# Digits laid out tile by tile, low parts of the first weights on VectorE, and a third place for stacked keys and queries

## The chip, the core and the metric

The kernel runs on one core of a Trainium2 chip. The metric is the device time of one execution in microseconds; a kernel's time is the median of its runs. The engines are TensorE (PE in the profile, its weight loads PEld), VectorE (DVE), ScalarE (ACT), GpSimd (POOL) and SyncE (SP), which issues most DMAs.

## What is computed

Three layers follow each other: attention with queries pooled in pairs (4 batches, 8 heads, 1152 positions, head width 64), a mixture of experts that gives each of 2304 tokens one of 8 experts with a capacity of 288 each, and a gated feed-forward layer of width 1536.

```python
q_pool = q.reshape(B, H, S // 2, 2, D).mean(axis=3)
scores = scale * np.matmul(q_pool, k.transpose(0, 1, 3, 2))
attn = softmax(scores)                      # over the keys
x = (attn @ v) as rows of [2304, 512]
flat = (x @ w_gate).flatten()               # 2304 x 8 logits
for idx in np.argsort(-flat):               # best pair first
    tok, e = idx // E, idx % E
    if assigned[tok] >= 0 or counts[e] >= cap: continue
    assigned[tok] = e; counts[e] += 1
out[mask_e] = relu(x[mask_e] @ w1[e]) @ w2[e]     # per expert
y = (silu(out @ w_gate2) * (out @ w_val)) @ w_out
```

## The kernel before

**Attention** is cut into units: one head of one batch with 576 pooled queries in batches 0 to 2, and in the last batch (`b == B - 1`) twice eight half-units, with 320 and then 256 queries (16 in all). For each of nine key tiles `score` (L351, L352) makes two matmuls into a PSUM bank, `expo` (L373) takes the exponential on ScalarE, `value` (L385) multiplies by the values, `add_weights` (L393, L395) adds the weights of three key tiles on GpSimd, and `sum_weights` (L400) sums them on TensorE into the same bank (`pv`, one buffer). `x_copy` (L414) and `den_copy` (L422) empty that bank. Scores are made in split precision: a stacked tile holds the high part of the keys in rows 64 to 127 twice and the low part in rows 0 to 63 (`ks`), and the queries lie likewise in `qs`, with the negative row maxima in its first two rows (`mrows_mm` L328, `mrows_copy` L333). `stack` (L252 to L256) fills such a tile by five DMAs, in the last batch from the scratch tensors `kh_s`, `kl_s` and `q_s` in DRAM. There are two places for stacked tiles; unit `u` uses place `u % 2`.

The order of all this is written out by a planner (`Plan`): each task has an engine, a duration, a due time, tasks that it comes after, buffers that it takes and frees, and a latency until another engine sees it. The planner always takes the task that can start first, the earliest due time among equals, and the engines' queues follow that order. A stack is a task of 2.0 on SP with a latency of 6.0 (`stlat`); it comes after the one before (`last_st`), and after the buffer is free. Scores of a unit come after its stack. VectorE has fillers: `rank_cmp` (L561, L563) compares one tile of 128 tokens with all tokens up to it for one expert, 2.7 planner microseconds for tile 12, and these are added only while tasks of attention are left.

**The tail** does the comparisons that were not placed: `tail_cmp` on VectorE (L993, L960) with 15 to 18 matmuls that count (L999), some by ScalarE. GpSimd prepares constants at the same time (`pool_steps`), among them `colv`, a grid of column numbers [128, 128, 18] with the token tile innermost.

**The routing rounds** (7 of them) find, for each expert, the rank up to which tokens are taken. A round takes each token's best key (`choose`), splits its rank in two digits, writes for each digit a table of thresholds `onehot` [128, digit value, token tile] by `is_ge` (`up_to`, L1163, four operations, two per digit), counts them by 18 matmuls per digit (`count`, L1171) with 8-column weights, and finds the cut (`cut`, L1177, L1179). Each matmul reads the columns `ths[k][:, :, i]`, which lie 18 elements apart. At the end of six rounds, `rows_after` turns a tile of rows and stores it to `x_rows`.

**Behind the rounds** the places of the tokens are split into digits again (`low_digit` L1267, `high_digit` L1273 and L1274) and 18 matmuls per list (`tokens_of`, L1281) give the gather indices `gidx0`, `gidx1` and the scatter indices `sidx`. `warm_up` (L1289) puts matmuls over 512 columns of `colv` between. Then GpSimd gathers the first expert's rows (L1344), TensorE transposes them (L1349), and the expert matmuls start (`hidden` L1418, `project` L1437).

**The expert weights** are loaded in pieces of 128x1024 (`w_load`, L1324) and split by `w_split`: ScalarE makes the high part (L1332), a subtraction the low part (L1334). The first three pieces are split early, right behind the tail, with both subtractions of each on GpSimd; of the later ones VectorE takes the first half and GpSimd the second.

Instructions outside `manual_schedule` are put in order when the program is built, by readiness and program order. `tc.issue_after(ins)` puts what it encloses behind `ins` on the same engine.

## Time and profile before

| what | us |
|---|---|
| median of 3 runs (1415.59 to 1419.45) | 1418.36 |
| the profiled execution | 1414.83 |
| its span, first to last instruction | 1413.0 |
| TensorE busy in the span | 1318.2 (93%) |
| VectorE busy | 938.4 (66%) |
| ScalarE busy | 612.5 (43%) |
| GpSimd busy | 520.8 (37%) |
| last attention batch, 461.0 to 609.3 | 148.3 |
| tail, 609.3 to 657.4 | 48.1 |
| routing rounds, 657.4 to 716.1 | 58.7 |
| digits and first gather, 716.1 to 728.7 | 12.6 |
| both expert layers, 728.7 to 1413.0 | 684.3 |

A row of the trace begins with the start in microseconds from the start of the span and the duration, then the engine, the line of the kernel, the operation, what is written and read, and the shape; in brackets stands the idle time of the engine before it and what ended that. Ends of matmuls are modelled, and spans on GpSimd are rough.

### The profile page before, as it was taken

The page shows a single profiled execution, that of the slowest core. Times are in us where ns is not written, and L with a number is a line of the kernel's source. Part 1 is how long each engine was busy: PE and PEld are TensorE (multiplying, and loading weights), DVE is VectorE, ACT ScalarE, POOL GpSimd, SP SyncE. Part 2 cuts the span into 40 slices and gives each one's busy share as a digit, 9 for nine tenths or more (in the row PEclk, how much of TensorE's full clock was granted, in tenths as well). Part 3 has the DMA queues.
Part 4 walks back from the last instruction along what each step waited for, and adds up shares of the span by engine and source line. Part 5 has one row for each costly group of instructions (what it writes and reads, how often), then busy time and mean ns, then how long its engine had stood idle before and what let it go on. Part 6 is the DMA issues. An engine that isn't in the chain of part 4 may idle for free.

```text
span 1413.0 us, 26870 instructions
## 1 busy us (share of the span) xinstructions
PE 1318.2 (93%) x10236; PEld 1095.4 (78%) x10237; DVE 938.4 (66%) x1960; ACT 612.5 (43%) x1643; POOL 520.8 (37%) x447
## 2 busy tenths in 40 slices
PE   7999999999999988786679999999999999999997
PEld 5565655666655777676569999999999999999997
DVE  5767688878989899979658888866742323232322
ACT  4556555555545555555226555654321212121211
POOL 7655323333324364553037677755610000000000
PEclk9999999999989999888569999999999999999999
DMA  7656566566643786621037767754310101010000
GB/s 223 190 155 185 134 173 188 126 179 180 188 93 88 194 211 160 155 76 46 38 101 244 241 231 244 255 189 129 90 45 1 45 1 45 1 45 0 23 0 23
DMA packets 78352, 174.43 MB, mean 123 GB/s; under 512 B 8448, under 2 KB 38160, under 8 KB 78224
## 3 DMA queue, kind: packets, MB, share of 16 engines
q1 hardware_dynamic: 75248, 163.29, 40.9%
q0 software_dynamic: 2976, 9.44, 1.8%
q8 instruction: 80, 1.31, 0.4%
q14 instruction: 48, 0.39, 0.1%
HBM read 120.86 MB, written 21.31 MB: 101 GB/s over the span
## 4 chain that ended last, share of the span: by engine, by line
PE 54%; DVE 18%; issue 17%; ACT 4%; POOL 2%; DMA 2%; SPq 1%; POOLq 0%; ACTq 0%; DVEq 0%
PE pv L385 8%; PE py L1437 7%; PE ph L1418 7%; PE st L351 6%; DVE cmp L561 6%; PE pm L282 4%; PE pg L1524 4%; PE misc L1524 4%; PE po L1547 4%; PE st L352 3%; PE pv L400 2%; DVE cmp L563 2%; PE pc L1171 2%; DVE cmp L993 1%; DVE mxp L294 1%
## 5 line engine op out<-in xcount | busy, mean ns | idle before, releaser
L294 DVE TENSOR_REDUCE mxp<-pm 128x1 f32<-128x384 f32 x405 | 199.5, 549 | 73.7 <-PE pm L282 70.7
L373 ACT ACTIVATE Lrow<-st 128x288 f32<-128x288 f32 (+2 forms) x432 | 154.3, 411 | 94.3 <-PE st L352 80.3
L351 PE MATMUL st<-qs,ks 128*128 128x288 f32 (+2 forms) x504 | 171.3, 352 | 9.9 <-ACT Lrow L373 7.0
L561 DVE SCALAR_TENSOR_TENSOR cmp<-Lrow,Lt,cmp 128x384 fp8e4<-128x384 f32 (+8 forms) x145 | 153.2, 1077 | 0.0
L352 PE MATMUL st<-qs,ks 128*128 128x288 f32 (+2 forms) x504 | 149.3, 306 | 3.3 <-ACT qs L333 3.2
L1555 POOL DMA_INDIRECT out_dram<-ot,si x18 | 17.4, 968 | 362.5 <-DVE ot L1552 359.9
L393 POOL TENSOR_TENSOR Lrow<-Lrow 128x576 f32<-128x576 f32 (+2 forms) x50 | 70.3, 1405 | 206.1 <-ACT Lrow L373 203.6
L1535 DVE TENSOR_TENSOR sg<-pg,sg 128x384 f32<-128x384 f32 x72 | 40.1, 556 | 159.4 <-ACT sg L1534 159.4
L351 PEld LDWEIGHTS st<-qs,ks 128*128 128x128 f32 x504 | 99.1, 197 | 49.6 <-ACT Lrow L373 23.7
L385 PE MATMUL pv<-Lrow,v 128*64 128x288 f32 (+2 forms) x900 | 124.9, 415 | 3.4 <-ACT den L422 3.2
L1334 POOL TENSOR_TENSOR wl<-wr,wh 128x512 fp32r<-128x512 f32 x67 | 103.5, 1551 | 59.0 <-ACT wh L1332 30.8
L352 PEld LDWEIGHTS st<-qs,ks 128*128 128x128 f32 x504 | 100.3, 199 | 4.8 <-ACT qs L333 4.8
L1534 ACT ACTIVATE sg<-pg 128x384 f32<-128x384 f32 x72 | 35.3, 491 | 155.4 <-PE pg L1524 155.4
L1537 ACT CAST ah<-ac 128x384 fp32r<-128x384 f32 x72 | 36.9, 513 | 149.2 <-DVE ac L1536 149.2
L1524 PE MATMUL pg<-yl,w2h 128*128 128x384 f32 x288 | 96.9, 337 | 0.1
L1524 PE MATMUL pg<-yh,w2h 128*128 128x384 f32 x288 | 97.0, 337 | 0.0
L1524 PE MATMUL pg<-yh,w2l 128*128 128x384 f32 x288 | 96.8, 336 | 0.0
L1524 PE MATMUL misc<-yh,w2h 128*128 128x384 f32 x288 | 96.8, 336 | 0.0
L1524 PE MATMUL misc<-yl,w2h 128*128 128x384 f32 x288 | 96.8, 336 | 0.0
L1524 PE MATMUL misc<-yh,w2l 128*128 128x384 f32 x288 | 96.8, 336 | 0.0
L385 PEld LDWEIGHTS pv<-Lrow,v 128*64 128x64 f32 x900 | 59.2, 140 | 46.7 <-issue 13.6
L1547 PE MATMUL po<-w2l,ah 128*128 128x512 f32 x216 | 85.5, 396 | 0.0
(281 smaller groups left out, 3465.4 us busy)
## 6 DMA issues: line engine op xcount, KB each, us to landing
wr<-in_wm_dram SPq DMA_DIRECT2D x64, 512.0 KB, 3.6
raw<-in_wm_dram SPq DMA_DIRECT2D x36, 512.0 KB, 4.1
ks<-pkh SPq DMA_DIRECT2D x23, 576.0 KB, 5.6
v<-in_v_dram SPq DMA_DIRECT2D x20, 576.0 KB, 6.3
pk<-in_kT_dram SPq DMA_DIRECT2D x16, 576.0 KB, 5.6
pq<-in_qT_dram SPq DMA_DIRECT2D x32, 288.0 KB, 6.4
Lrow<-l_cols SPq DMA_DIRECT2D x18, 512.0 KB, 5.6
ks<-kh_s SPq DMA_DIRECT2D x16, 576.0 KB, 7.3
```

What stands on the lines that cost most here:

```text
L294: nc.vector.tensor_reduce(mx[:, i, j:j + 1], p[:, :w3], axis=AX.X, op=OP.max)
L351: nc.tensor.matmul(p[:, :w], KS[u][:, 1, ks], QS[u][:, 1, cs_], start=True, stop=False)
L352: nc.tensor.matmul(p[:, :w], KS[u][:, 0, ks], QS[u][:, 0, cs_], start=False, stop=True)
L373: nc.scalar.activation(EX[u, gi, kt][:, ti * w:(ti + 1) * w], ST.pop((u, gi, kt, ti))[:, :w], AF.Exp, scale=SCALE)
L385: nc.tensor.matmul(p[64 * k:64 * k + 64, :hn], VT[u][:, kt, o:o + 64], ex[:, k * hn:(k + 1) * hn], start=(kt == 0), stop=(kt == KT - 1), s ...
L393: nc.gpsimd.tensor_add(w[:, :n], a, b)
L561: nc.vector.scalar_tensor_tensor(c[:, sl], Lrow[:, e, sl], Lt[:, i, e:e + 1], c[:, sl], op0=OP.is_ge, op1=OP.add, accum_out=acc, saturate= ...
L1334: eng.tensor_sub(WL[k][:, s], r[:, s], WH[k][:, s].bitcast(F32))
L1418: nc.tensor.matmul(p[:, :CAP], w[:, cs_], x[:, c, :], start=(n == 0), stop=(n == 11))
L1437: nc.tensor.matmul(PY[e][m][:, :CAP], w[:, ms], h, start=(f == 0 and n == 0), stop=(f == FB1 - 1 and n == 2))
L1524: nc.tensor.matmul(p[:, :TG], w[ft][:, cs_], y[g][:, c, :], start=(n == 0), stop=(n == 11))
L1547: nc.tensor.matmul(PO[g][t], a[:, ts], w[ft][:, 1024:], start=(ft == 0 and n == 0), stop=(ft == FB2 - 1 and n == 2))
```

## The change

Attention: the planner gets a third kind of place, `ks3`, for every third unit of the last batch. It is made of the `kh` and `qh` tiles of two slots in which batches 0 to 2 prepared keys and queries; two memsets on GpSimd set its constant rows. Stacks of the last batch no longer come after the stack before.

Routing: `onehot` is [128, token tile, digit value], so the columns that a matmul reads are neighbours, and `colv` is one row of 128 numbers. The source that holds the digits is repeated over the innermost dimension. `warm_up` reads `onehot`.

Weights: the three early splits are made in rounds 1, 3 and 5, their subtractions on VectorE behind the `nbelow` reductions of this round and the one before.

```diff
+    U3 = next(u for u in range(NU) if units[u][0] == B - 1)
+    third = [u >= U3 and (u - U3) % 3 == 1 for u in range(NU)]
+    place = [sum(not x for x in third[:u]) % BUFS["ks"] for u in range(NU)]
+    def KS(u, k):
+        return slots[1 - k]["kh"] if third[u] else ksbuf[place[u]][:, k]
+    def QS(u, k):
+        return slots[1 - k]["qh"] if third[u] else qsbuf[place[u]][:, k]
+    def third_init():
+        nc.gpsimd.memset(KS(U3 + 1, 0)[:64].bitcast(F32), 1.0)
+        nc.gpsimd.memset(QS(U3 + 1, 0)[:64].bitcast(F32), 0.0)
...
-        nc.sync.dma_start(ks[64:], kh[:, None].to_broadcast([64, 2, S]))
+        if third[u]:
+            for k in range(2):
+                nc.sync.dma_start(ks[k][64:], kh)
+        else:
+            nc.sync.dma_start(ksbuf[place[u]].bitcast(F32)[64:], kh[:, None].to_broadcast([64, 2, S]))
...
+        if u == U3 + 1:
+            ks3_init = [add("POOL", 3.0, up - 16, third_init, (), (buf("prep0"), buf("prep1")))]
...
-            kdep = [add("SP", 2.0, up + PRM["k2due"], lambda u=u, t=t: stack(u, t), ready + last_st, (bks,),
+            kdep = [add("SP", 2.0, up + PRM["k2due"], lambda u=u, t=t: stack(u, t), ready + (last_st if u <= U3 else []) + (ks3_init if third[u] else []), (bks,),
...
-    colv = rst.tile([128, 128, NT], I16, name="colv")
+    colv = rst.tile([128, 128], I16, name="colv")
-    onehot = rst.tile([128, 128, NT], BF, name="onehot")
+    onehot = rst.tile([128, NT, 128], BF, name="onehot")
...
-        for k in range(4):
-            nc.gpsimd.iota(colv[:, k * 32:(k + 1) * 32], pattern=[[1, 32], [0, NT]], base=32 * k, channel_multiplier=0)
-            yield
+        nc.gpsimd.iota(colv, pattern=[[1, 128]], base=0, channel_multiplier=0)
+        yield
...
-            nc.vector.tensor_tensor(ths[k][:, :, sl], grid[:, :n, sl],
-                                    digs[k][:, None, sl].to_broadcast([128, n, HT]), op=OP.is_ge)
+            nc.vector.tensor_tensor(ths[k][:, sl], colv[:, None, :n].to_broadcast([128, HT, n]),
+                                    digs[k][:, sl, None].to_broadcast([128, HT, n]), op=OP.is_ge)
...
-            nc.tensor.matmul(p[:E, :n], who[:, i, :], ths[k][:, :, i], start=(i == 0), stop=(k == 0 and i == NT - 1))
+            nc.tensor.matmul(p[:E, :n], who[:, i, :], ths[k][:, i, :], start=(i == 0), stop=(k == 0 and i == NT - 1))
...
-            eng = nc.vector if a == 0 and not early else nc.gpsimd
-            eng.tensor_sub(WL[k][:, s], r[:, s], WH[k][:, s].bitcast(F32))
+            if early:
+                with tc.issue_after(early[a].ins):
+                    nc.vector.tensor_sub(WL[k][:, s], r[:, s], WH[k][:, s].bitcast(F32))
+            else:
+                eng = nc.vector if a == 0 else nc.gpsimd
+                eng.tensor_sub(WL[k][:, s], r[:, s], WH[k][:, s].bitcast(F32))
...
+            ins = nc.vector.tensor_reduce(nbelow, below.rearrange("p i e -> p e i"), axis=AX.X, op=OP.add)
+        told.append(ins)
+        if rnd % 2 and rnd < 2 * WAH:
+            w_split(rnd // 2, told[-2:])
+            w_load(rnd // 2 + LAH - WAH)
...
-            nc.vector.tensor_tensor(ob[:, :, a:b], colv[:, :, a:b], lo[:, None, a:b].to_broadcast([128, 128, b - a]),
-                                    op=OP.is_equal)
+            nc.vector.tensor_tensor(ob[:, a:b], colv[:, None].to_broadcast([128, b - a, 128]),
+                                    lo[:, a:b, None].to_broadcast([128, b - a, 128]), op=OP.is_equal)
...
-            nc.tensor.matmul(p, identb, colv[:, :32].rearrange("p a i -> p (a i)")[:, :512].bitcast(BF), start=True, stop=True)
+            nc.tensor.matmul(p, identb, junk[:, :512], start=True, stop=True)
```

`high_digit`, `tokens_of` and the threshold slices `ths` follow the new layout in the same way.

## Rows read from the trace of the kernel before

**Rows 1.** Busy time per engine in two stretches: PE, PEld, DVE, ACT, POOL, clock, DMA.

```profile
461.00:609.30 148.30, 124.53 (x1691) 103.79 (x1691) 131.81 (x255) 80.74 (x284) 76.29 (x64) 0.92 0.72 172
671.30:716.10 44.80, 30.74 (x263) 24.33 (x262) 28.76 (x120) 10.50 (x48) 0.00 (x0) 0.50 0.19 71
```

**Rows 2.** Timeline of TensorE in the last attention batch.

```profile
461.03 0.41 PE L351 MATMUL st<-qs,ks 128*128 128x320 f32 x1
...
462.98 1.68 PE L385 MATMUL pv<-Lrow,v 128*64 128x288 f32 x12
...
513.16 0.41 PE L351 MATMUL pm<-qs,ks 128*128 128x320 f32 x1
...
517.64 1.85 PE L385 MATMUL pv<-pk,v 128*64 128x160 f32 x24 [1.34 <-ACT den L422]
...
521.30 0.41 PE L351 MATMUL st<-qs,ks 128*128 128x320 f32 x1
```

**Rows 3.** Timeline of SyncE: the first DMA of a stack.

```profile
507.79 0.44 SPq L252 DMA_DIRECT2D ks<-kl_s  x1
```

**Rows 4.** TensorE's waits, 473.7 to 609.4: us in total, times, longest.

```profile
PE pv L400 <- POOL pq L395: 6.7, 5, 2.2
PE pv L385 <- ACT den L422: 5.2, 4, 1.5
...
PE pm L352 <- ACT qs L333: 2.6, 4, 1.1
```

**Rows 5.** VectorE by line in the tail: count, busy us, mean ns, idle before.

```profile
L993 DVE TENSOR_SCALAR cmp<-Lrow,Lt 128x2176 fp8e4<-128x2176 f32 (+4 forms) x26 | 33.2, 1276 | 0.0
L960 DVE SCALAR_TENSOR_TENSOR cmp<-Lrow,Lt,tri 128x128 fp8e4<-128x128 f32 x31 | 10.7, 353 | 0.6 <-PE csum L956 0.6
```

**Rows 6.** Timelines of GpSimd and VectorE around the first round.

```profile
657.40 7.79 POOL L1334 TENSOR_TENSOR wl<-wr,wh 128x512 fp32r<-128x512 f32 x6 [0.79 <-ACT wh L1332]
...
657.74 1.09 DVE L1126 TENSOR_TENSOR key<-key,R 128x144 f32<-128x144 f32 x1
658.76 1.30 DVE L1130 CAST Ri<-R 128x144 int16<-128x144 f32 x1
...
671.29 0.30 DVE L1153 TENSOR_REDUCE best<-key 128x18 f32<-128x144 f32 x1
```

**Rows 7.** VectorE by form in the six later rounds, 671.3 to 716.

```profile
L1163 DVE TENSOR_TENSOR onehot<-colv,dig 128x576 bf16<-128x576 int16 x12 | 7.0, 584 | 0.0
...
L1163 DVE TENSOR_TENSOR onehot<-colv,dig 128x324 bf16<-128x324 int16 x12 | 3.9, 396 | 0.0
...
L1156 DVE TENSOR_TENSOR dm<-key,best 128x144 bf16<-128x144 f32 x6 | 1.8, 301 | 0.0
```

**Rows 8.** Timeline of one round, TensorE's counts and VectorE's cuts.

```profile
702.30 1.36 PE L1171 MATMUL pc<-onehot,dm 128*8 128x36 bf16 x18 [0.77 <-DVE onehot L1163]
...
703.70 0.18 DVE L1177 SCALAR_TENSOR_TENSOR under<-pc,onesb 8x36 bf16<-8x36 f32 x1 [0.45 <-PE pc L1171]
...
704.88 2.26 PE L1171 MATMUL pc<-onehot,at_cut 128*8 128x64 bf16 x18 [0.47 <-DVE at_cut L1209]
...
707.23 0.21 DVE L1177 SCALAR_TENSOR_TENSOR under<-pc,onesb 8x64 bf16<-8x64 f32 x1 [1.75 <-PE pc L1214]
```

**Rows 9.** TensorE by form in the same six rounds.

```profile
L1171 PE MATMUL pc<-onehot,at_cut 128*8 128x64 bf16 x108 | 13.5, 294 | 2.8 <-DVE at_cut L1209 2.8
...
L1214 PE MATMUL pc<-onesb,nbelow 128*8 128x64 bf16 x6 | 1.4, 233 | 0.0
```

**Rows 10.** VectorE: the later weight subtractions (least, median, most ns), and `low_digit`.

```profile
L1334 DVE TENSOR_TENSOR wl<-wr,wh x61: 674/693/1652, 735.1 to 947.5; 128x512 fp32r<-128x512 f32 x61
...
L1267 DVE TENSOR_TENSOR onehot<-colv,place 128x768 f16<-128x768 int16 x3 | 1.6, 555 | 0.0
```

**Rows 11.** Timeline behind the rounds: the second `low_digit` and the matmuls of `sidx`.

```profile
723.66 1.35 DVE L1267 TENSOR_TENSOR onehot<-colv,place 128x2304 f16<-128x2304 int16 x1
...
726.30 1.24 PE L1281 MATMUL pc<-small,onehot 128*128 128x18 f16 x18
```

More of the change, by code (lines that the diff above doesn't have):

```diff
@@ L192, in fused_attention_moe_kernel @@
     qsbuf = [atp.tile([128, 2, NQ], F32R, name=f"qs{i}") for i in range(BUFS["ks"])]
-    KS = [ksbuf[u % BUFS["ks"]] for u in range(NU)]
-    QS = [qsbuf[u % BUFS["ks"]] for u in range(NU)]
     mxbuf = [atp.tile([128, 5, 3], F32, name=f"mx{i}") for i in range(2)]
@@ L250, in stack @@
             ql, qh = [q_s[h // 2, r, k, q0:q0 + n] for k in range(2)]
-        ks, qs = KS[u].bitcast(F32), QS[u].bitcast(F32)
-        nc.sync.dma_start(ks[:64, 1], kl)
-        nc.sync.dma_start(ks[64:], kh[:, None].to_broadcast([64, 2, S]))
-        nc.sync.dma_start(qs[64:, 0, :n], ql)
+        ks, qs = [KS(u, k).bitcast(F32) for k in range(2)], [QS(u, k).bitcast(F32) for k in range(2)]
+        nc.sync.dma_start(ks[1][:64], kl)
+        if third[u]:
[3 more added lines that the diff above has]
+            nc.sync.dma_start(ksbuf[place[u]].bitcast(F32)[64:], kh[:, None].to_broadcast([64, 2, S]))
+        nc.sync.dma_start(qs[0][64:, :n], ql)
         for k in range(2):
-            nc.sync.dma_start(qs[64 * k:64 * k + 64, 1, :n], qh)
+            nc.sync.dma_start(qs[1][64 * k:64 * k + 64, :n], qh)
     def load_v(u):
@@ L332, in mrows_copy @@
         c0, end = ts[0][2], ts[-1][2] + ts[-1][3]
-        nc.scalar.copy(QS[u][0:2, 0, c0:end], p[:2, :end - c0])
+        nc.scalar.copy(QS(u, 0)[0:2, c0:end], p[:2, :end - c0])
     EX, PV, ST, SW = {}, {}, {}, {}
@@ L350, in score @@
         cs_ = slice(c0 + ti * w, c0 + (ti + 1) * w)
-        nc.tensor.matmul(p[:, :w], KS[u][:, 1, ks], QS[u][:, 1, cs_], start=True, stop=False)
-        nc.tensor.matmul(p[:, :w], KS[u][:, 0, ks], QS[u][:, 0, cs_], start=False, stop=True)
+        nc.tensor.matmul(p[:, :w], KS(u, 1)[:, ks], QS(u, 1)[:, cs_], start=True, stop=False)
+        nc.tensor.matmul(p[:, :w], KS(u, 0)[:, ks], QS(u, 0)[:, cs_], start=False, stop=True)
     def weights(b, kind):
@@ L949, in fused_attention_moe_kernel @@
     eskip = rst.tile([128, NT, E], F32, name="eskip")
-    onehot = rst.tile([128, 128, NT], BF, name="onehot")
-    junk = onehot.rearrange("p a i -> p (a i)")
+    onehot = rst.tile([128, NT, 128], BF, name="onehot")
+    junk = onehot.rearrange("p i a -> p (i a)")
     acc = pcs.tile([128, 512], F32, name="csum")
@@ L1069, in fused_attention_moe_kernel @@
         acts, pools = act_cmps(), pool_steps()
-        na, np_ = 5 * len(by_act), 27
+        na, np_ = 5 * len(by_act), 24
         for i in last:
@@ L1139, in fused_attention_moe_kernel @@
     digs = [sm(f"dig{k}", [128, NT], I16) for k in range(2)]
-    ths = [onehot[:, :GH], onehot[:, GH:GH + GL]]
+    ths = [onehot[:, :, :GH], onehot[:, :, 64:64 + GL]]
     hd = sm("hd", [128, NT, E], BF)
@@ L1190, in rows_after, with w_load, w_split @@
             tok_store(i)
+    WR, WH, WL = {}, {}, {}
+    NPC = E * FB1
+    def w_load(k):
+        WR[k] = m1r.tile([128, 1024], F32, name="wr")
+        nc.sync.dma_start(WR[k], wm1[k // FB1, k % FB1])
+    def w_split(k, early=()):
+        r = WR.pop(k)
+        WH[k] = m1w.tile([128, 1024], F32R, name="wh")
+        WL[k] = m1w.tile([128, 1024], F32R, name="wl")
+        for a in range(2):
+            s = slice(a * 512, a * 512 + 512)
+            nc.scalar.copy(WH[k][:, s], r[:, s])
+            if early:
[4 more added lines that the diff above has]
+                eng.tensor_sub(WL[k][:, s], r[:, s], WH[k][:, s].bitcast(F32))
+    with ExitStack() as after:
+        for ins in tail:
+            after.enter_context(tc.issue_after(ins.ins))
+        for k in range(LAH - WAH):
+            w_load(k)
+    told = []
     for rnd in range(E - 1):
@@ L1211, in fused_attention_moe_kernel @@
         with nc.allow_low_precision("counts up to NT"):
-            nc.vector.tensor_reduce(nbelow, below.rearrange("p i e -> p e i"), axis=AX.X, op=OP.add)
+            ins = nc.vector.tensor_reduce(nbelow, below.rearrange("p i e -> p e i"), axis=AX.X, op=OP.add)
[3 more added lines that the diff above has]
+            w_load(rnd // 2 + LAH - WAH)
         p = count(1, at_cut)
@@ L1318, in fused_attention_moe_kernel @@
     moctx.enter_context(tc.manual_schedule())
-    WR, WH, WL = {}, {}, {}
-    NPC = E * FB1
-    def w_load(k):
-        WR[k] = m1r.tile([128, 1024], F32, name="wr")
-        nc.sync.dma_start(WR[k], wm1[k // FB1, k % FB1])
-    def w_split(k, early=False):
-        r = WR.pop(k)
-        WH[k] = m1w.tile([128, 1024], F32R, name="wh")
-        WL[k] = m1w.tile([128, 1024], F32R, name="wl")
-        for a in range(2):
-            s = slice(a * 512, a * 512 + 512)
-            nc.scalar.copy(WH[k][:, s], r[:, s])
-            eng = nc.vector if a == 0 and not early else nc.gpsimd
-            eng.tensor_sub(WL[k][:, s], r[:, s], WH[k][:, s].bitcast(F32))
     XG, XH, XL = {}, {}, {}
@@ L1464, in fused_attention_moe_kernel @@
     n_early = 4 * 3 * NW2A
-    with ExitStack() as after:
-        for ins in tail:
-            after.enter_context(tc.issue_after(ins.ins))
-        for k in range(LAH - WAH):
-            w_load(k)
-        for k in range(WAH):
-            w_split(k, True)
-            w_load(k + LAH - WAH)
     for n in range(3):
```

20 lines of the change are left out of this document (10 added, 10 removed).

## The prediction, made before the changed kernel ran

> **What bounds the kernel now.** I read the stage table first [rows 1], then the order of TensorE, SyncE and VectorE inside the two stages that the diff touches. The page puts TensorE at 93% of the span and the chain that ended last at 54% TensorE, but that is an average over stages with different limits. Two stretches carry this change.
>
> The last attention batch runs from 461.0 to 609.3 us. TensorE is busy for 124.53 of 148.3 us there at a mean granted clock of 0.92 [rows 1], so it idles for 23.8 us. The reader should see how a unit is laid out [rows 2]: the scores of one half-unit start at 513.16, its values (`value`, L385) at 517.64 after 1.34 us of waiting for ScalarE's denominator copy, and the scores of the next unit only at 521.30, when the values are over. A unit takes 521.30 - 513.16 = 8.1 us and nothing of two units overlaps on TensorE. The keys are not what it waits for: the SyncE issue at 507.79 [rows 3] is the stack for the unit that begins at 521.30. The order comes from the planner. It holds each stack of the last batch to the landing of the stack before (`last_st`): 2.0 of issue plus `stlat` 6.0 are 8.0 planner microseconds per unit, which is the 8.1 of the trace. The waits that this order leaves are TensorE's 6.7 us for GpSimd's weight sums, 5.2 us for the denominator copy and 2.6 us for the row of maxima [rows 4]: 14.5 us.
>
> From 657.4 on the routing rounds are one serial chain between VectorE and TensorE. Six rounds take 44.8 us at a granted clock of 0.50, which is the 1.2 GHz level [rows 1], so 7.47 us each. From the first operation on `key` at 657.74 to the end of the first round at 671.29 [rows 6] it is 13.55 us.
>
> **Part 1, GpSimd's six subtractions leave the first round.** They run from 657.40 for 7.79 us [rows 6]. In that time VectorE's small operations take four times as long: `key` 1.09 us and `Ri` 1.30 us for 144 elements [rows 6], where a two-source operation on 144 elements takes 301 ns later [rows 7]. The 13.55 us hold one round (7.47), `key` and `Ri` (at 0.3 each) and two operations on `high` that only the first round has (0.4 together, an estimate from the same 301 ns). What is left is the price of the sharing: 13.55 - 7.47 - 0.6 - 0.4 = **5.1 us gained**. Late next is VectorE's own chain at its usual durations. Bounds 4 to 5.6.
>
> **Part 2, the subtractions on VectorE.** One of 128x512 f32 costs 693 ns on VectorE undisturbed (674 at the least) [rows 10]. `issue_after` puts each behind a `nbelow` reduction, one per round in rounds 0 to 5. There VectorE waits 1.75 us for the second count [rows 8]. That cover shrinks by the 1.10 us of part 3 to 0.65, so each sticks out by some 0.05: **0.3 us lost**. Queued behind it on VectorE is `cut(1)`, and TensorE's next small matmul waits for that. If the scheduler sets them elsewhere, all six lie on the path: 6 x 0.69 = 4.2 us. Their weight casts on ScalarE fall in the rounds or in the tail's gaps, and the three later weight loads on SyncE now wait for a subtraction, with the `x_rows` store of the same round behind them; that store comes later in the round anyway. GpSimd's next work is the gather. I cost these moves at nothing; a cast that holds a row copy up would be part of the 4.2.
>
> **Part 3, the rounds with the new layout.** Per round the thresholds are written by four VectorE operations and read by 18 + 18 matmuls.
> TensorE: 18 matmuls over 64 columns take 2.26 us and 18 over 36 columns 1.36 us [rows 8], so (2.26 - 1.36)/(18 x 28) = 1.79 ns per column. These columns lie 18 elements apart. One matmul of the same 8-column weights over 64 neighbouring columns takes 233 ns, the strided one 294 [rows 9]: 61 ns less each. In the new layout the columns are neighbours, so the second count loses 18 x 0.061 = 1.10 us and the first, by 36/64 of that, 0.6. Below 69 ns a pair of load and matmul isn't seen in this stage (18 in 1.24 us, with 128-column weights [rows 11]); if the pace stops there the gain is 0.85 in place of 1.10.
> The Trainium skill, TensorE: Matmul & The Clock Gate, section "Wait — 56ns, not 53.3ns?", gives the pace in the cold state as the columns over 1.2 GHz with no term for the layout, and some 62 ns of sequencer time per matmul; by it 64 columns would go at 62 ns already and this edit would buy nothing on TensorE (a rival, below). The 2.26 us row speaks against it.
> VectorE: the digit becomes a source that stands still over the innermost dimension. Two ends: at one element per cycle, from 144 elements in 301 ns and 512 in 693, 1.065 ns per element and 148 ns fixed, so 576 elements cost 0.76 us and 324 cost 0.49; at two per cycle, from 768 in 555 ns [rows 10], 0.45 and 0.32. Today they cost 0.584 and 0.396 [rows 7]. I take the slow end: `dm` [rows 7] is the row nearest in pattern, with one source repeated over the last dimension, though its sources are 4 bytes wide.
> The Trainium skill, Vector Engine (DVE) Microarchitecture Reference, section 5.1, says that one element read 16 times as a source of a two-source operation with 2-byte operands ran at one per cycle on trn2. By it the slow end holds; no row here shows such an operation.
> At the slow end the path of a round goes so. The three operations ahead of `cut(0)` add 0.10 + 0.10 + 0.18 = 0.38; VectorE idles 0.45 there now [rows 8], TensorE's count is done earlier, so 0.07 is gained. The second half of `up_to(1)` stands ahead of `at_cut`: 0.18 lost. The second count: 1.10 gained. Together 1.0 us a round, 7 rounds: **7.0 us gained**. At the fast end: 0.6 for the first count, 0.13 for the operation before `at_cut`, 1.10: 1.83 a round, 12.8 us. Lower bound, with the pace of 69 ns: 0.75 a round, 5.2.
>
> **Part 4, the digits behind the rounds.** The three pieces of `low_digit` go from 555 to 148 + 1.065 x 768 = 966 ns, 1.2 us on the path to the first gather; its matmuls win back some 0.2. The second `low_digit` (1.35 us, started at 723.66 [rows 11]) becomes 2.60, and it overwrites `onehot`, which the five warm-up matmuls now read: it waits for them. The 18 matmuls of `sidx` (at 726.30 [rows 11]) stand ahead of eight of the twelve transposes of the first gather; if they stay there they hold them up by one more microsecond, if the scheduler moves them back they don't. **1.5 us lost**, bounds 0.3 gained (fast end) to 3 lost.
>
> **Part 5, the third place.** With a third place and without the chain of stacks, the planner can start the scores of a unit while the unit before is at its values, as it did at 461.03, where the first unit's scores precede the last values of batch 2 [rows 2]. I take two thirds of the 14.5 us of waits, 9.7. The mean clock of 0.92 over 148.3 us is 11.9 us of work that the low level cost; a quarter of it sits behind those waits by estimate: 3. Together **12.7 us gained**; ends 0 (ScalarE, GpSimd or the DMA queues bind in place of the planner's order) and 20. The transfers stay the same bytes; the third place adds one SyncE issue to its units and two GpSimd memsets in batch 2, beside GpSimd's idle time.
> It costs something behind: VectorE's comparisons (`rank_cmp`) are fillers that the planner adds only while attention lasts. By its own costs attention takes 16 x 8.0 = 128 for the last batch, and without the chain what TensorE's tasks take, some 7.5 and 6.3 for the two kinds of unit and 11 for token tiles, 121.5: 6.5 less, at 2.7 a filler about 3 fillers. Each turns up in the tail as one comparison of 1276 + 353 ns [rows 5], some 0.17 of it overlapped by estimate, 1.46 us on VectorE, which sets the tail's pace: **4.4 us lost**, bounds 0 to 12.
>
> **The sum.** 5.1 - 0.3 + 7.0 - 1.5 + 12.7 - 4.4 = 18.6 us. The profiled execution took 1414.83 us (1413.0 of span and 1.8 around it), which gives 1396.2. It lies 3.5 us under the median of the runs, 1418.36; a median is what is forecast: 1418.36 - 18.6, **1400 us**.
>
> **The rivals.**
> *Attention gives it back.* ScalarE is busy for half of the last batch and GpSimd likewise, and each unit's copies are serial; if the net of part 5 is nothing, the 10.3 us of parts 1 to 4 remain: 1408. For it: the waits for GpSimd [rows 4] would stay if its additions are late by themselves. Against it: the 8.1 us unit that equals the planner's 8.0.
> *Two elements per cycle.* Parts 3 and 4 win 5.8 and 1.8 more: 1392. Against it: the digit source has no neighbour to be read with.
> *TensorE gains nothing from neighbouring columns.* Then 7 x 1.1 is missing: 1408. Against it: 233 beside 294 ns.
> *Slower: the fillers.* If the planner's clock for the last batch shrinks by far more than the chip's, many comparisons fall into the tail and attention isn't shorter. Place: the stretch after 609.3; price 1.46 us each; from 7 it eats parts 1 to 4, from 10 with no gain in attention the kernel is slower than before by 0.3%, at 13 it stands at 1418.4 - 10.3 + 19.0 = 1427. For it: 26 comparisons stand in the tail now [rows 5], and a filler that isn't placed is in the tail for certain. Against it: 6.5 planner microseconds are 3 fillers.
>
> **How the numbers follow.** Forecast 0.60 (own range 1392 to 1406), attention gives it back 0.20, two per cycle 0.08, TensorE nothing 0.07, fillers 0.05. The range 1387 to 1411 takes in the first four with the bounds of parts 2 and 4, and leaves out the fillers and the ends of two bounds meeting. About 0.3% (4.3 us) is what a measurement of this kernel can tell from no change, so faster means under 1414.1. The first four cases lie under that except for a tail of the second and the fourth: faster 0.90, same 0.06, slower 0.04.
>
> **What would show it.** Step by step in the profile after: the first round as long as the others and `key` near 0.3 us (part 1); six `wl` subtractions of about 0.69 us on VectorE in the rounds and a round of about 6.5 us (parts 2 and 3); 18 matmuls over 64 columns in about 1.15 us; thresholds of 576 elements at 0.76 us, or 0.45 for the rival; the first gather about 1 us later after the last round; in the last batch scores of a unit ahead of the values of the one before, and the stage near 136 us in place of 148.3; 29 comparisons in the tail in place of 26. Wrong would be: the 8.1 us unit unchanged, thresholds at 0.45 us, over 33 comparisons in the tail, or VectorE's `cut(1)` waiting behind the new subtractions.

## The result, and the profile after

The changed kernel takes 1399.6 us in the median of its runs (1399.2 to 1402.4) beside 1417.0 for the kernel before on the same chip (1414.3 to 1419.5): a ratio of 0.988, with a 95% interval of 0.986 to 0.990, so some 17 us or 1.2% less. Its profiled execution took 1399.8 us, 1398.0 of them span. The forecast was 1400. The sum is right, but not every term of it is: three stages missed by more than 3 us, in both directions, and that they cancel is luck.

The stage table is read from the two timelines. Each stage ends with one named instruction: the first 128x320 score of the last batch, the last weight sum of attention, the first work on `key` (`key` plus `R`), the eighth `choose`, the first `hidden` matmul.

| stretch | before | after | difference | forecast |
|---|---|---|---|---|
| start to the first score of the last batch | 461.0 | 465.7 | +4.7 | 0 |
| last attention batch | 148.3 | 129.9 | -18.4 | -12.7 |
| tail, up to `key` | 48.4 | 56.8 | +8.4 | +4.4 |
| `key` to the eighth choice | 58.4 | 45.9 | -12.5 | -11.8 |
| digits, up to the first `hidden` matmul | 12.6 | 14.9 | +2.3 | +1.5 |
| the rest | 684.3 | 684.8 | +0.5 | 0 |

Busy time per engine in the two stretches of the changed kernel that answer to [rows 1] (columns as there):

```profile
465.70:595.60 129.90, 117.64 (x1688) 99.66 (x1688) 127.44 (x238) 80.17 (x283) 85.63 (x64) 0.95 0.82 187
658.90:698.20 39.30, 21.23 (x265) 16.11 (x264) 35.68 (x127) 10.50 (x48) 0.00 (x0) 0.50 0.31 106
```

In the last batch TensorE idles for 12.3 us in place of 23.8, and its busy time is 6.9 us less at a granted clock of 0.95 in place of 0.92. In the rounds the clock stands at the same level as before, VectorE is busy for 91% of the time, and it was for 64%: the chain is now mostly VectorE's.

What TensorE waits for in the last batch, longest first, against [rows 4]:

```profile
PE pm L540 <- DVE Lt L510: 6.8, 2, 5.8
PE st L367 <- ACT den L438: 1.7, 1, 1.7
PE pv L401 <- ACT den L438: 1.6, 5, 0.6
...
PE pv L416 <- POOL pq L411: 0.7, 1, 0.7
```

The 6.7 us for GpSimd's weight sums have become 0.7, the 5.2 for the denominator copy 3.3, the row of maxima is gone. What is late now is the logits of a token tile, 6.8 us in two waits (2.8 before), with VectorE busy for 127.4 of 129.9 us. In the kernel before VectorE had run out of work for the last 12.7 us, up to its first operation of the tail:

```profile
610.25 0.57 DVE L1067 COPY small<-ident8f 128x576 int32<-128x576 int32 x1 [12.67 <-POOL small L1063]
```

In the changed kernel it has work up to the end of attention. The prediction did not name VectorE among what could bind the batch; it is now about as long as VectorE's own work.

The timeline of TensorE shows why its waits went; this is the stretch that answers to [rows 2]:

```profile
498.90 0.30 PE L368 MATMUL pm<-qs,ks 128*128 128x320 f32 x1
499.04 0.38 PE L367 MATMUL st<-pqh,pkh 128*128 128x320 f32 x1
...
500.83 1.85 PE L401 MATMUL pv<-pk,v 128*64 128x160 f32 x24
...
505.55 0.42 PE L367 MATMUL pm<-pqh,pkh 128*128 128x320 f32 x1
```

At 499.04 the scores of the next unit, read from the third place (`pqh`, `pkh`), follow the scores of the unit before without a gap, and the values of the unit before come only behind them, at 500.83. Counted over the trace, twelve of the last batch's sixteen units start their values behind 6 to 12 score matmuls of the next unit. The kernel before did this too, but for two units of sixteen and with 6 matmuls each. The scores that begin at 521.30 in [rows 2] belong to the first of the two, and these of the next unit stand ahead of its values:

```profile
524.64 0.41 PE L351 MATMUL pm<-qs,ks 128*128 128x320 f32 x1
...
526.14 1.85 PE L385 MATMUL pv<-pk,v 128*64 128x160 f32 x24
```

So "nothing of two units overlaps" in the prediction holds for the unit that it shows, and not for every one.

One round of the changed kernel, against [rows 8]:

```profile
659.37 0.30 DVE L1169 TENSOR_REDUCE best<-key 128x18 f32<-128x144 f32 x1
...
660.01 0.89 DVE L1179 TENSOR_TENSOR onehot<-colv,dig 128x324 bf16<-128x324 int16 x2
660.55 0.83 PE L1187 MATMUL pc<-onehot,dm 128*8 128x36 bf16 x18 [0.85 <-DVE onehot L1179]
...
661.12 0.75 DVE L1179 TENSOR_TENSOR onehot<-colv,dig 128x576 bf16<-128x576 int16 x1
...
663.18 1.12 PE L1187 MATMUL pc<-onehot,at_cut 128*8 128x64 bf16 x18 [0.69 <-DVE at_cut L1253]
...
663.70 0.68 DVE L1224 TENSOR_TENSOR wl<-wr,wh 128x512 fp32r<-128x512 f32 x1
...
664.40 0.21 DVE L1193 SCALAR_TENSOR_TENSOR under<-pc,onesb 8x64 bf16<-8x64 f32 x1
...
665.85 0.30 DVE L1169 TENSOR_REDUCE best<-key 128x18 f32<-128x144 f32 x1
```

The round takes 665.85 - 659.37 = 6.48 us in place of 7.47. The second count is 1.12 us (2.26 before), a threshold of 576 elements 0.75 (0.584 before), and the weight subtraction ends at 664.38, just when the second count's last matmul does, so `cut(1)` at 664.40 waits for neither. The first round begins with

```profile
652.41 0.31 DVE L1142 TENSOR_TENSOR key<-key,R 128x144 f32<-128x144 f32 x1
652.64 0.23 DVE L1146 CAST Ri<-R 128x144 int16<-128x144 f32 x1
```

where [rows 6] had 1.09 and 1.30 us beside GpSimd's subtractions.

The tail, VectorE's two costliest lines (last column: idle time ahead of them), against [rows 5]:

```profile
L1010 DVE TENSOR_SCALAR cmp<-Lrow,Lt 128x2176 fp8e4<-128x2176 f32 (+4 forms) x29 | 35.6, 1228 | 6.1 <-PE prw L1016 4.0 <-PE csum L973 2.1
L977 DVE SCALAR_TENSOR_TENSOR cmp<-Lrow,Lt,tri 128x128 fp8e4<-128x128 f32 x34 | 11.4, 346 | 0.0
```

There are 29 comparisons, the three more that were forecast. What was not forecast is the 6.1 us that VectorE waits for TensorE there; the same two lines waited 0.6 us before. The digits, last, against [rows 11]:

```profile
705.00 1.35 POOL L1376 DMA_INDIRECT xg<-x_rows,gi  x1 [53.87 <-DVE dr L1352]
...
708.02 0.88 POOL L1376 DMA_INDIRECT xg<-x_rows,gi  x1 [0.30 <-issue]
708.14 2.56 DVE L1315 TENSOR_TENSOR onehot<-colv,place 128x2304 f16<-128x2304 int16 x1 [0.74 <-PE prw L1338]
...
710.41 1.68 PE L1381 MATMUL py<-identf,xg 128*128 128x128 f32 x8 [0.51 <-DMA xg<-x_rows,gi]
...
712.02 0.65 PE L1330 MATMUL pc<-small,onehot 128*128 128x18 f16 x18
712.75 1.31 ACT L1387 CAST xh<-py 128x288 fp32r<-128x288 f32 x4 [18.80 <-PE pc L1330]
```

The first gather starts 6.73 us after the eighth choice (5.72 before). The second low digit takes 2.56 us and waits 0.74 us for the warm-up matmuls that read `onehot`, as the prediction said. The `sidx` matmuls now stand behind all twelve transposes, and ScalarE's casts wait for them.

### The profile page after: what moved, and what is told of

Same layout as the page of the kernel before. It is cut to its first block, busy times and chain, and to the rows that moved or that the text cites. A ratio compares the mean times of both kernels' runs of the same rounds, so it can differ in the third digit from the quotient of the medians.

```text
span 1398.0 us, 26982 instructions
## 1 busy us (share of the span) xinstructions
PE 1310.6 (94%) x10287; PEld 1088.1 (78%) x10287; DVE 943.3 (67%) x1960; ACT 612.9 (44%) x1644; POOL 518.5 (37%) x442
## 4 chain that ended last, share of the span: by engine, by line
PE 63%; issue 17%; DVE 12%; ACT 3%; DMA 3%; POOL 2%; SPq 1%; ACTq 0%; POOLq 0%; DVEq 0%
PE pv L401 10%; PE py L1469 7%; PE st L367 6%; PE ph L1450 6%; PE pg L1548 6%; PE misc L1548 6%; PE po L1571 5%; PE pm L298 4%; PE st L368 4%; PE pv L416 3%; DVE cmp L577 3%; DVE cmp L1010 1%; DVE onehot L1179 1%; DVE cmp L579 1%; PE pm L481 1%
## 5 line engine op out<-in xcount | busy, mean ns | idle before, releaser
L367 PE MATMUL st<-qs,ks 128*128 128x288 f32 (+2 forms) x482 | 165.3, 355 | 8.9 <-ACT Lrow L389 6.4
L577 DVE SCALAR_TENSOR_TENSOR cmp<-Lrow,Lt,cmp 128x384 fp8e4<-128x384 f32 (+9 forms) x142 | 152.3, 1092 | 0.0
L368 PE MATMUL st<-qs,ks 128*128 128x288 f32 (+2 forms) x482 | 142.4, 306 | 2.7 <-ACT qs L349 2.6
L367 PEld LDWEIGHTS st<-qs,ks 128*128 128x128 f32 x482 | 94.6, 196 | 48.7 <-ACT Lrow L389 23.5
L401 PE MATMUL pv<-Lrow,v 128*64 128x288 f32 (+2 forms) x900 | 127.4, 422 | 3.4 <-ACT den L438 3.2
L1227 POOL TENSOR_TENSOR wl<-wr,wh 128x512 fp32r<-128x512 f32 x61 | 95.6, 1571 | 60.1 <-ACT wh L1221 33.0
L368 PEld LDWEIGHTS st<-qs,ks 128*128 128x128 f32 x482 | 95.7, 199 | 3.7 <-ACT qs L349 3.7
```

What stands on the lines that cost most here:

```text
L367: nc.tensor.matmul(p[:, :w], KS(u, 1)[:, ks], QS(u, 1)[:, cs_], start=True, stop=False)
L368: nc.tensor.matmul(p[:, :w], KS(u, 0)[:, ks], QS(u, 0)[:, cs_], start=False, stop=True)
L401: nc.tensor.matmul(p[64 * k:64 * k + 64, :hn], VT[u][:, kt, o:o + 64], ex[:, k * hn:(k + 1) * hn], start=(kt == 0), stop=(kt == KT - 1), s ...
L577: nc.vector.scalar_tensor_tensor(c[:, sl], Lrow[:, e, sl], Lt[:, i, e:e + 1], c[:, sl], op0=OP.is_ge, op1=OP.add, accum_out=acc, saturate= ...
L1227: eng.tensor_sub(WL[k][:, s], r[:, s], WH[k][:, s].bitcast(F32))
```

## The experiments

All are timed beside runs of the kernel before on the same chip; that one's median was 1417.3 for the first four, 1416.3 for the next four and 1418.9 for the last three.

**The routing part alone, the attention part alone.** The first is the kernel before with the new layout of the digits and the moved subtractions; the second is the kernel before with only the edits of places and chain, of which this is the line of the chain:

```diff
-            kdep = [add("SP", 2.0, ..., lambda u=u, t=t: stack(u, t), ready + last_st, (bks,),
+            kdep = [add("SP", 2.0, ..., lambda u=u, t=t: stack(u, t), ready + (last_st if u <= U3 else []) + (ks3_init if third[u] else []), (bks,),
```

> The kernel before with the digits laid out tile by tile and the six subtractions on VectorE, and with the attention part left as it was (two places, the chain of stacks). If the parts add up as the two traces say, the stretch from the first work on the keys to the eighth choice takes 45.9 us in place of 58.4 and the digits 14.9 in place of 12.6, so 10.2 us less than the kernel before: 1407 against 1417. The tail (from the end of attention to the keys) stays at 48.4 us with 26 comparisons. If instead attention had given back what it won, this kernel alone would stand at the 1400 of the changed one. And if the 4.7 us by which the changed kernel reaches its last batch later come from the attention part, they are missing here: the first score of the last batch is at 461.0, as before.

> The kernel before with the third place and without the chain of stacks in the last batch, the routing left as it was. If the parts add up: the last batch 130 us in place of 148.3, the tail 56.6 in place of 48.4 with 29 comparisons, and 0 to 4.7 us lost ahead of the last batch: 5.3 to 10 us less than before, 1407 to 1412. If attention gives back what it wins: 1417. The first round takes 13.55 us again, a later one 7.47.

Routing alone: 1405.9 us, a ratio of 0.993 (0.990 to 0.996). Attention alone: 1410.1 us, 0.995 (0.993 to 0.998). That is 11.4 and 7.2 us off the median, and the two ratios add to 16.4 us where the whole change has 17. By stages, routing alone has 45.8 us from `key` to the eighth choice, 15.0 for the digits, a last batch of 147.8 and a tail of 47.9; attention alone has a last batch of 129.6, a tail of 56.8 and the 58.5 us of routing as before. So the parts add up within the spread of the runs, and the tail's extra 8 us belong to the attention part. "Attention gives it back" has fallen: it keeps 7 of its 18 us.

**Which edit of the attention part.** The prediction laid the 8.1 us unit to the chain of stacks. Two kernels take the edits apart: the changed kernel with two places and no chain, and the changed kernel with the third place and the chain:

```diff
-    third = [u >= U3 and (u - U3) % 3 == 1 for u in range(NU)]
+    third = [False] * NU
```

```diff
-... ready + (last_st if u <= U3 else []) + (ks3_init if third[u] else []), (bks,),
+... ready + last_st + (ks3_init if third[u] else []), (bks,),
```

> The changed kernel with two places for stacked keys and queries, as before, and still without the chain of stacks in the last batch. My prediction laid the 8.1 us unit to the chain: by that theory the last batch stays near 130 us and the time near 1400. The rival is the place: with two, a stack has to wait until the scores of the unit two before it are over, and that alone keeps the order as it was. By the planner's own costs the plan then ends 1.3 us before that of the kernel before (the changed kernel's 12.1 before it), and 26 comparisons are left for the tail as before. By the rival: the last batch 146 to 148 us, the tail 48 and the time 1407, as with the routing part alone.

> The changed kernel with its third place, and with the chain that holds each stack to the landing of the one before kept in the last batch too. If the chain bound the kernel before, as my prediction has it, nothing is won in attention: last batch 148 us and a time of 1407 or more. If the place did, most of the gain stays: by the planner's costs the plan ends 8.0 us before that of the kernel before in place of 12.1, so two thirds of the 18 us, a last batch of some 136 us with 28 comparisons in the tail, and 1402 to 1405.

Two places without the chain: 1403.9 us (ratio 0.992, 0.990 to 0.995). The third place with the chain: 1403.5 us (0.992, 0.990 to 0.994). The last batch of each, busy time per engine as above, first the one with two places:

```profile
462.10:607.80 145.70, 124.36 (x1694) 103.79 (x1695) 132.25 (x255) 79.82 (x284) 80.13 (x64) 0.93 0.74 175
```

```profile
463.30:597.90 134.60, 119.54 (x1691) 100.02 (x1691) 128.56 (x247) 81.29 (x284) 80.05 (x64) 0.95 0.77 181
```

Without the chain but with two places the batch takes 145.7 us, 2.6 less than before. With the third place and the chain it takes 134.6, 13.7 less. So the place carries three quarters of the 18.4 us. Taking the chain away as well gives the last 4.7, and without the place 2.6. These two are no larger than the spread: the nine kernels here that have the place and no chain took 127.0 to 131.7 us for the batch, so 134.6 lies only 2.9 us above their longest. The order agrees: with two places and no chain three units of sixteen have scores of the next ahead of their values, with the place and the chain eight do. The tails are 47.3 and 54.9 us, so the gain in attention and the loss in the tail come together. The times of these two kernels are nearly alike in part because of that.

**Pairs of tiles.** The changed kernel with the digit layout [pair of tiles][value][tile of the pair], so that the digit source has two neighbours innermost and TensorE's columns lie 2 elements apart:

```diff
-    colv = rst.tile([128, 128], I16, name="colv")
+    colv = rst.tile([128, 128, 2], I16, name="colv")
...
-    onehot = rst.tile([128, NT, 128], BF, name="onehot")
+    onehot = rst.tile([128, NT // 2, 128, 2], BF, name="onehot")
...
-            nc.tensor.matmul(p[:E, :n], who[:, i, :], ths[k][:, i, :], ...
+            nc.tensor.matmul(p[:E, :n], who[:, i, :], ths[k][:, i // 2, :, i % 2], ...
```

> The changed kernel with the digits laid out by pairs of tiles: the two tiles of a pair are neighbours in memory, the values of the digit come next, so that the digit source has two neighbouring elements in its innermost dimension, and TensorE reads columns that lie 2 elements apart. By the theory that the digit source alone, which stands still over the innermost dimension, holds VectorE at one element per cycle, thresholds of 640 and 512 elements take 0.49 and 0.42 us (in place of 0.75 for 576), the half ahead of the second count wins 0.33 us a round and the work ahead of the first cut some 0.3 to 0.5, the low digit's pieces fall from 0.95 to 0.55 us: 5 to 7 us in all, 1393 to 1395. Rival one: a second source of 2 elements is no better, then 0.81 and 0.68 us and 1400. Rival two: TensorE pays for every step above one element, then 18 matmuls over 64 columns take between 1.12 us (neighbours) and 2.26 (18 elements apart), and each tenth costs 0.7 us over seven rounds.

It takes 1388.8 us, a ratio of 0.980 (0.979 to 0.982): 27 us under the kernel before and 11 under the changed one. Its round, the thresholds and the second count:

```profile
661.46 0.48 DVE L1180 TENSOR_TENSOR onehot<-colv,dig 128x640 bf16<-128x640 int16 x1
...
662.25 0.41 DVE L1180 TENSOR_TENSOR onehot<-colv,dig 128x512 bf16<-128x512 int16 x1
...
662.96 1.12 PE L1189 MATMUL pc<-onehot,at_cut 128*8 128x64 bf16 x18 [0.40 <-DVE at_cut L1255]
```

640 elements take 0.48 us where 576 took 0.75. With the prediction's 148 ns of fixed cost that is 0.52 ns per element in place of 1.04, its two elements per cycle with two neighbours in the digit source and its one without. TensorE takes 1.12 us for columns 2 elements apart, as for neighbours. A round is 5.58 us, 0.90 less; `key` to the eighth choice is 39.5 us (-6.3) and the digits are 13.2 (-1.7). The Trainium skill, Vector Engine (DVE) Microarchitecture Reference, section 5.1, has both sides of this: one element read 16 times as a source of a two-source operation with 2-byte operands ran at one per cycle, and the packed mode wants more than one element in the innermost dimension. These rows agree with it.

**The tail's wait.** Two kernels for two causes. One sums four of the open comparison chains ahead of the tail, which frees their buffers:

```diff
-            if k % 2 == 0 and k // 2 < len(rest):
-                x = rest[k // 2]
+            for x in (rest[:4] if k == 0 else rest[k + 3:k + 4]):
```

The other keeps TensorE at work in the tail's first wait:

```diff
         tok_logits(*last)
+        keep_warm(prw.tile([128, 512], F32, name="prw"), 36)
         for i in last:
```

> The changed kernel with four of the seven open comparison chains summed by TensorE ahead of the tail's first comparison, in the 3 us in which it waits for VectorE's logits, and the others one per step. Two causes are possible for the 6.1 us that VectorE waits in the tail (0.6 before): seven of eight comparison buffers are still held by chains whose sums have not run (five before), or TensorE's clock is at 1.2 GHz there. By the buffers the waits of 1.23, 2.30 and 1.72 us go, the tail falls from 56.8 to 52 or 53 us and the time to 1395 to 1397. By the clock the waits stay as they are, within half a microsecond: 1399 to 1400.

> The changed kernel with 36 matmuls of 128 columns on ones, whose result nobody reads, on TensorE ahead of the two broadcasts of the logits in the tail, where it waits 3.1 us. By the clock theory the granted clock between 600 and 612 us is then 1.0 in place of 0.5 to 0.6, 14 matmuls of a comparison take 1.07 us in place of 1.91, and VectorE's waits fall by 2 to 3 us: 1396 to 1398. By the buffer theory only the first of the waits falls by the 0.8 us of faster matmuls and the rest stays: 1399.

Early sums: the tail takes 51.8 us in place of 56.8, and VectorE's waits there fall from 6.5 us in all to 3.0; none of them is for `prw` any more:

```profile
DVE small L1083 <- POOL small L1079: 1.4, 1, 1.4
DVE cmp L1010 <- PE csum L973: 1.2, 1, 1.2
DVE R L1133 <- PE csum L973: 0.4, 1, 0.4
```

Warm: 55.3 us, waits of 4.2 us, with these clocks ahead of and in the stretch where the changed kernel had 0.53:

```profile
597.00:602.00 5.00, 3.90 (x70) 3.64 (x70) 3.33 (x13) 1.65 (x5) 4.38 (x12) 1.00 0.00 0
602.00:612.00 10.00, 7.51 (x95) 7.14 (x92) 7.81 (x13) 4.24 (x12) 4.33 (x12) 0.66 0.77 261
```

The 1.4 us for `small` cost nothing: VectorE copies it 0.9 us behind the end of attention in both kernels, and was only done earlier with its work for attention here. So the waits that count fall by 4.8 us, nearly all of the 5.0. The early sums also keep TensorE at work in that first wait, so they could have acted by the clock. They did not at first: the counts of the first two comparisons still take 1.91 and 1.86 us, and VectorE passes them without waiting.

```profile
602.79 1.91 PE L1016 MATMUL prw<-small,cmp 128*128 128x146 fp8e4 x14
...
603.61 1.07 DVE L1010 TENSOR_SCALAR cmp<-Lrow,Lt 128x1664 fp8e4<-128x1664 f32 x1
```

In the changed kernel VectorE waited 2.30 and 1.72 us for counts of 1.91 and 1.88 us there. So the buffers are the larger cause (5.0 us of the tail). The clock is the smaller (1.5; it rose only in part), and the two can't simply be added, since faster counts free buffers sooner as well. The times are less plain: 1397.3 us (ratio 0.986, 0.984 to 0.989) and 1400.1 (0.990, 0.987 to 0.993) beside 1399.6. Both profiles lost 1.9 us in the digits, 16.8 in place of 14.9, which is taken up below.

**The subtractions back on GpSimd.** Parts 1 and 2 undone, with the three splits right behind the tail again:

```diff
-                with tc.issue_after(early[a].ins):
-                    nc.vector.tensor_sub(WL[k][:, s], r[:, s], WH[k][:, s].bitcast(F32))
+                nc.gpsimd.tensor_sub(WL[k][:, s], r[:, s], WH[k][:, s].bitcast(F32))
...
```

> The changed kernel with the six early weight subtractions back on GpSimd, right behind the tail as in the kernel before. It undoes parts 1 and 2 alone. By my prediction they are worth 5.1 - 0.3 = 4.8 us: the stretch from the keys to the eighth choice grows from 45.9 to 50.7 us, the first work on the keys takes 1.1 us in place of 0.3, and the time is 1404. If the six subtractions on VectorE cost as much as GpSimd's did, 1400. If VectorE waited in the rounds anyway and they cost nothing, 5.1 more: the later rounds stay at 6.48 us or fall by less than 0.1.

It takes 1405.8 us (0.992, 0.989 to 0.995). From `key` to the eighth choice it is 51.9 us in place of 45.9, and the first round shows why:

```profile
650.47 7.93 POOL L1223 TENSOR_TENSOR wl<-wr,wh 128x512 fp32r<-128x512 f32 x6 [1.08 <-ACT wh L1221]
650.67 1.22 DVE L1142 TENSOR_TENSOR key<-key,R 128x144 f32<-128x144 f32 x1
...
656.80 1.96 DVE L1179 TENSOR_TENSOR onehot<-colv,dig 128x324 bf16<-128x324 int16 x2
```

Parts 1 and 2 are worth 6.1 us here, 1.3 more than forecast: the first thresholds also fall beside GpSimd's work, 1.96 us in place of 0.89. The later rounds take 6.48 us with the subtractions and without them. The digits have 16.8 us in this kernel too, so of the 6.2 us between its median and the changed kernel's some may be that and not parts 1 and 2.

**The third gather.** With the new layout tile by tile the digits take 14.9 to 15.0 us in four profiles and 16.8 in three. In the kernel with early sums, one of the three:

```profile
703.94 2.56 DVE L1314 TENSOR_TENSOR onehot<-colv,place 128x2304 f16<-128x2304 int16 x1 [0.51 <-PE prw L1337]
704.04 3.21 POOL L1375 DMA_INDIRECT xg<-x_rows,gi  x1 [0.30 <-issue]
```

In the changed kernel the gather began 0.12 us ahead of the 2.56 us operation and took 0.88 us; here it began 0.10 behind it and took 3.21. Two kernels cut that operation into three, one with the layout by pairs and early sums and one with the early sums alone; a third has pairs and early sums uncut:

```diff
-        low_digit(lo, (0, NT))
+        low_digit(lo, (0, 6, 12, NT))
```

> The layout by pairs and the early sums of the chains together. If the two gains add up (10.8 us of the pairs, 5.0 us off the tail's 56.8), the tail takes 52 us, a round 5.58 us and the time is 1384, or up to 1387 where GpSimd's third gather again waits for VectorE. If the early sums only move a wait into the rounds: 1389.

> The kernel with pairs and early sums, and the second low digit, one VectorE operation of 2304 elements (1.36 us), in three of 768. In the runs so far GpSimd's third gather issue took 0.88 us where it began before that operation and the operation's length plus 0.65 us where it began behind it (3.21 against 2.56, 2.03 against 1.36). If GpSimd is held for the length of one VectorE operation, the third issue takes 1.2 us or less here and the digits stage 0.5 to 0.9 us less than with one operation: 1383. If VectorE's next piece holds it again, 2.0 as before and the same time.

> The changed kernel with the early sums and its second low digit (2.56 us in one operation) in three operations of 0.95 us. In the kernel with early sums alone the third gather took 3.21 us and the digits stage 16.8 us in place of 14.9. If GpSimd is held for the length of one VectorE operation, the third issue takes 1.6 us or less and the stage 15.0 to 15.3: 1395 to 1396. If it is held as long as VectorE has such work in a row, 3.2 and 16.8 again: 1397.

The cut kernel with early sums alone:

```profile
699.84 0.95 DVE L1314 TENSOR_TENSOR onehot<-colv,place 128x768 f16<-128x768 int16 x1
700.66 0.88 POOL L1375 DMA_INDIRECT xg<-x_rows,gi  x1 [0.30 <-issue]
```

The issue takes 0.88 us and the stage 14.95 us. It began 0.12 us ahead of the end of that piece and ended 0.75 us behind it, though VectorE went on to other operations with two sources, the second piece among them at 701.11. In the uncut kernel with early sums the issue also ended 0.75 us behind the end of the operation beside which it began (707.25 for 706.50), and with pairs too (704.32 for 703.57). So GpSimd's issue is held to the end of one VectorE operation, not for the stretch of them. That is read from one profile of the cut kernel, in which the issue met only the end of a piece. This kernel takes 1396.5 us (ratio 0.985, 0.981 to 0.988). With pairs the two took 1387.0 us uncut (0.979, 0.975 to 0.983) and 1388.0 cut (0.978, 0.975 to 0.982). Uncut, the gather happened to begin ahead of the operation (0.88 us), so the cut had nothing to win there, and the stage is 13.1 and 13.2 us. The tails are 53.8 and 52.1 us in place of the 57.0 of pairs alone, but beside its 1388.8 neither time can be told from it: the early sums' gain in the tail is seen in the profiles and not in these medians. The 1384 expected was not reached.

## Why the prediction was right, point by point

**Part 1** was forecast at 5.1 us. The first round took 13.55 us before, 6.08 more than a later one; now it takes 6.96, 0.48 more. So 5.6 us are gained, the upper bound. The term that was mis-sized: `key`, `Ri` and `high` were set at 1.0 us that stays, and 0.48 stay.

**Part 2** was forecast at 0.3 us lost. The last round, which has no subtraction, takes 6.49 us and those with one 6.48: they cost nothing. The cover was there nearly as reckoned (VectorE waits 0.61 us in the last round, 0.65 forecast) and the operation took 0.68.

**Part 3** was forecast at 1.0 us a round by its slow end. It is 0.99, with the terms as worked out: the second count 1.12 us (1.15), thresholds 0.75 and 0.49 (0.76 and 0.49). The kernel by pairs shows the rival's two elements per cycle and what they were worth; they need a neighbour in the digit source, which is what spoke against that rival. That TensorE gains nothing from neighbouring columns has fallen with 2.26 to 1.12 us. The 62 ns of sequencer time per matmul that the prediction quotes for this rival did not bind here: 18 matmuls over 36 columns passed in 0.83 us, 46 ns each. Nor did the pace of 69 ns under its lower bound: the 18 pairs of `sidx` from which it was read take 0.65 us now in place of 1.24, and both of their operands had a step before. That bound was also mis-added: at 69 ns a pair 2.26 us become 1.24, a gain of 1.02 and not 0.85.

**Part 4** was forecast at 1.5 us lost, and 2.3 were. The first gather is 1.0 us later, as reckoned. The mis-sized term is what lies behind it: the scheduler did move `sidx` behind the transposes, but ScalarE's casts then wait for `sidx` (0.65 us). Most of the other 0.7 us is TensorE's clock: the last eight transposes take 1.68 us at a granted clock of 0.50 (the 1.2 GHz level), and before they took 1.00 at 1.00 (the 2.4 GHz level):

```profile
727.40 1.00 PE L1349 MATMUL py<-identf,xg 128*128 128x128 f32 x8
```

The prediction had no term for the clock in this stage. In other kernels here the second digit's 2.56 us cost 1.9 more, by the third gather.

**Part 5** was forecast at 12.7 us gained and 4.4 lost. The stage it named was the right one and the step that failed is its cause: the chain of stacks (`last_st`) did not set the 8.1 us unit. That the planner's 8.0 for the chain equals it was a coincidence of the unit that was read: the five units from 557.14 to 602.60 of the kernel before take 7.0, 11.4, 8.9, 9.2 and 9.0 us under the same chain. With two places the order stays nearly the same without the chain (145.7 us), since a stack needs the place that the scores of two units before it have left. The third place, to which the prediction gave no price of its own, carries 13.7 of the 18.4. The size was off too: the idle time fell by 11.5 us (9.7 forecast), and the busy time by 6.9, where 3 had been given to the clock.

The tail's three comparisons came as forecast, and its two lines of comparisons hold 3.1 us more than before, where 4.4 were reckoned. The term that was missed is the waits: VectorE waits 6.5 us for TensorE in the tail in place of 0.8. The planner's shorter attention leaves out not only fillers but sums of finished chains: 16 sum matmuls ran inside attention in place of 48, so seven chains hold seven of the eight comparison buffers when the tail starts, where five did. The early sums show this by giving 5.0 us of the tail back.

**Ahead of the last batch** nothing was forecast and 4.7 us were lost. The order of the instructions on every engine is the same there in both kernels but for two GpSimd memsets and, at its end, the loads of the next unit and its row of maxima, which come earlier. The timelines part most between 45 and 55 us, where TensorE has the same work; its busy time and clock there, before and after:

```profile
45.00:55.00 10.00, 10.00 (x58) 0.90 0.32 128
```

```profile
45.00:55.00 10.00, 10.00 (x37) 0.50 0.39 157
```

At the 1.2 GHz level fewer of the same matmuls are done, and 3.7 us of the 4.7 are lost by 80 us. The kernel with two places, which has neither the third place nor its memsets, shows the same stretch:

```profile
45.00:55.00 10.00, 10.00 (x36) 0.50 0.30 120
```

Over the profiles of all kernels here the first score of the last batch stands between 461.0 and 467.4 us. Routing alone has 461.1 and attention alone 467.4, but with the third place in them the kernel with early sums and the cut has 461.8 and the kernel by pairs 467.4, so the third place alone doesn't set it. The three kernels without it all lie low (461.0 to 462.1, against 461.8 to 467.4 for the ten with it), so that it has no part at all isn't shown. I take it for a spread between executions that follows the granted clock; what starts the low stretch in one and not in the other stays open.

The sum thus came out by luck, because a gain in attention 5.7 us larger than forecast met 4.0 us more loss in the tail and 4.7 in a place where none was due. The range of 1387 to 1411 was wide enough for each of these alone.

## What to carry to other kernels

When a unit's time equals a planner's constant, look for a second limit of the same size before pricing the first: here two buffers gave the same order as the chain. Work that a planner adds only while a stage lasts leaves two things behind when the stage gets shorter, the work itself and the buffers that it holds. When a layout is turned for one engine, try the halfway layout as well: pairs gave TensorE its close columns and VectorE its two elements per cycle.

## What the runs showed of the hardware that I had not expected

- GpSimd's issue of an indirect DMA is held while one VectorE operation with two SBUF sources runs: the third gather takes 0.88 us when it begins first, 3.21 beside an operation of 2.56, 2.03 beside one of 1.36. A tenth or two of a microsecond in who begins first decides 1.9 us of a stage. The Trainium skill, GPSIMD Engine Reference, section 8, says that GpSimd shares its SBUF interfaces with VectorE and is in contention with operations that have two SBUF inputs; these rows agree and give the size.
- TensorE reads columns 2 elements apart as fast as neighbours (1.12 us for 18 matmuls over 64 columns, at the 1.2 GHz level), and columns 18 elements apart at half that pace (2.26).
- The runs of one kernel spread by 9 us and more, and the spread follows the mean granted clock: of fourteen runs of the kernel before, the three shortest (1413.7 to 1413.9 us) had 0.949 to 0.950 and the three longest (1422.5 to 1422.9) 0.942 to 0.945. Which of the two is the cause isn't shown. The stretch ahead of the last batch, where no edit changes the order but at its end, differed by up to 6.4 us between profiles.
